# Branch B's weight folds: a block-diagonal matmul replaced by 32x32 tiles of the array, a turn on VectorE and a block exchange through DRAM

## The chip, the cores and the metric

The kernel runs on one core of one Trainium2 chip. The metric is the device time in microseconds of the whole program, as a median over several runs. A core has five engines with a queue each, and each works through its own list strictly in the order of the program: TensorE (PE, matmuls; its weight loads are listed as PEld), VectorE (DVE), ScalarE (ACT), GpSimd (POOL) and SyncE (SP, which here only issues DMAs). Matmul results lie in PSUM, which GpSimd and DMAs do not use here; all else lies in SBUF (128 partitions) or DRAM.

## The reference

Two attention branches A and B work on the same `x` (2048 rows of 448) with different weights, and their outputs are mixed by a gate per row. Cut to what matters here, one branch is

```python
qkv = (x @ wqkv).reshape(B, S, 3, H, Dh)            # D = 448, H = 16 heads of Dh = 28
pq = jnp.einsum("bhsd,hdf->bhsf", q, w_phi)          # per head, 28 x 28
pk = jnp.einsum("bhsd,hdf->bhsf", k, w_phi)
phi_q = concat([softmax(pq), softmax(-pq)])
phi_k = concat([softmax(pk), softmax(-pk)])
kv = jnp.einsum("bhsf,bhsd->bhfd", phi_k, v);  z = phi_k summed over s
o = (phi_q @ kv) / (phi_q @ z + 1e-6)
branch = o @ wo
out = sigmoid(x @ gate_w) * A + (1 - sigmoid(x @ gate_w)) * B
```

Since `q` and `k` are used only through `w_phi`, the kernel never computes them. It multiplies the weights first: for each head, `wqkv`'s 448x28 columns of that head times the head's 28x28 `w_phi`. This product is called a fold. There are four: k and q of branch A, k and q of branch B. The folded weights, 448x448 each, then stand in for the raw ones in the projections of `x`.

## The kernel before, in words

**Precision.** Projections run on pairs of a high and a low part (`fp32r` each). The high part of a tensor is a ScalarE copy into `fp32r`, the low part is the original minus the high part (VectorE or GpSimd). The 448 input channels are held as three chunks of 128 and one of 64 that stands twice in a tile of 128 partitions.

**Stages.** `x` is worked in 8 units of 256 rows (`NU = 8`, loop variable `u`). A first loop over `u` runs branch A's keys and values: `proj` with the folded k weights `wk[0]` (L446), `k_shift` and `k_exp` for both softmaxes (L195 to L202), `k_sums` (L211, L212 on VectorE and L220 on GpSimd) for their normalisation, `proj` with the values' weights (L459), `v_out` (L228), and `kv_acc` (L245), which adds unit `u - 1` to the state on TensorE. In the gaps it prepares branch B's weights: the split of `wv` and of `wo` into high and low parts (L131, L134) and the folds. A second loop over `u` runs branch B's keys and values with `wk[1]` and `wvs[1]`, and at the same time branch A's queries: `q_front` (L272, L274) stores them to DRAM in another order (`qd`), `q_load` reads them back (`tq`), `q_exp0`, `q_min`, `q_exp1` make both softmaxes (L297, L305, L312), `q_turn` (L315) turns 32x32 blocks on VectorE, `num` (L327) multiplies with the state in 32x32 tiles, and `a_turn`, `n_rec`, `n_den`, `weights`, `n_mul`, `n_add` (L522, L339 to L369) divide and weigh. A last part, ordered by the table STEPS, does branch B's queries and the output.

**Order.** Nothing is scheduled: each engine executes in the order in which the code issues. An instruction that waits holds all later ones of its engine; so do SP's DMAs.

**PSUM.** `two_tile()` hands out three tiles of two banks in rotation. Every projection, each half of a fold and each half of a `num` takes one, and TensorE must wait until the user of three takings ago has been read.

**A fold before** (`fold`, L159). `load_wt` brings the transposed raw weights of 4 heads at a time as 112 partitions, in four groups `g`. `bd` holds, for both branches, `w_phi` of the 4 heads of each group as a 112x112 block diagonal (built once on VectorE, L399). For each chunk of 128 channels and each group a matmul has the raw weights as the stationary operand and `bd` as the moving one (L151): 16 matmuls with 112 moving columns, in two PSUM tiles. `fold_out` then takes the high part on ScalarE (L156) and the low part on VectorE (L157) right from PSUM.

Branch B's k fold stands at the end of `u == 3` in the first loop (L492) and works on `wtb[1]`; its q fold stands in the second loop at `u == 0` (L563), between the projections of k and v, and works on a tile `ctr`. Both tiles are shared: `wtb` also holds pieces of `wo` (7 pieces of 32 rows per head group, `wo_part`, L409; `high_wo`, `low_wo`, stored to `wod`) and later the turned queries. `wk[1]` is first used by the projection of the second loop's `u == 0`, `wq[1]` by that of its `u == 6`.

## Time and profile before

| what | value |
|---|---|
| median of 3 runs | 353.95 us (353.79 to 353.97) |
| the profiled execution's own time | 353.85 us |
| its span in the profile | 352.1 us |
| granted TensorE clock | 1.0 |
| busy: PE / PEld / DVE / ACT / POOL | 345.7 / 305.9 / 271.6 / 121.7 / 261.9 us |
| branch B's k fold, L151 from 58.27 to the next group's start | 3.60 us |
| branch B's q fold, L151 from 116.71 to the next group's start | 3.56 us |

All times inside a run are microseconds from the start of the span. A row of the timeline gives the start, the length, the engine, the line of the kernel, the operation, output and inputs by the program's names, their shapes, and how many instructions were merged; a bracket tells how long the engine stood idle just before and what released it. In the page's last parts a row gives a group's busy time and mean. A matmul in full fp32 leaves two records.

### The profile page before, as it was taken

Reading aid. Unit: us, or ns where it says so; the run is one execution under the profiler, and the core shown is the slowest. Engines: PE = TensorE matmul, PEld = TensorE weight load, DVE = VectorE, ACT = ScalarE, POOL = GpSimd, SP = SyncE. Lnnn points to the kernel's source line nnn. Section 1 sums busy time; section 2 is a strip of 40 time slices with the busy share of each in tenths; the row PEclk is TensorE's granted clock in tenths of the full one; section 3 lists DMA queues with packets and bytes.
Section 4 is the critical chain, followed back from the end, with each engine's and each line's share of the span. In section 5 each row is a group of like instructions: output and inputs, shape, how many; then the busy total and the mean of one; then the engine's idle time right before and its main releaser. Section 6 shows DMA issues by size and latency. Waiting matters only on the chain.

```text
span 352.1 us, 8447 instructions
## 1 busy us (share of the span) xinstructions
PE 345.7 (98%) x3599; PEld 305.9 (87%) x3599; DVE 271.6 (77%) x313; ACT 121.7 (35%) x172; POOL 261.9 (74%) x228
## 2 busy tenths in 40 slices
PE   8999999999999999999999999999999999999994
PEld 7999889988899988889898988889888888888993
DVE  4428763852878859799989889898999999988840
ACT  5524444335145242324414141421125445343330
POOL 2553799597777206998988888895779999999840
PEclk9999999999999999999999999999999999999999
DMA  8796225511950303132233313178770553654111
GB/s 237 230 327 181 104 75 171 188 58 65 266 161 10 107 6 108 54 106 87 73 104 108 92 67 106 55 254 299 209 201 35 182 158 92 176 155 130 54 53 52
DMA packets 33877, 45.75 MB, mean 130 GB/s; under 512 B 11424, under 2 KB 27152, under 8 KB 33552
## 3 DMA queue, kind: packets, MB, share of 16 engines
q1 hardware_dynamic: 28688, 41.09, 37.5%
q10 hardware_dynamic: 5152, 4.13, 3.7%
q8 instruction: 28, 0.46, 0.5%
q14 instruction: 9, 0.07, 0.1%
HBM read 27.29 MB, written 19.53 MB: 133 GB/s over the span
## 4 chain that ended last, share of the span: by engine, by line
PE 81%; POOL 9%; DVE 5%; issue 1%; DMA 1%; ACT 1%; SPq 0%; POOLq 0%; ACTq 0%; DVEq 0%
PE two L181 50%; PE out L774 17%; PE two L327 5%; POOL e L220 3%; PE kv L245 3%; PE two L151 3%; POOL xg L112 2%; PE two L390 2%; DMA wtb<-wos 1%; DVE sm L211 1%; POOL e L198 1%; POOL wvb L134 1%; PE kv L327 1%; DVE wva L705 1%; POOL wtb L134 1%
## 5 line engine op out<-in xcount | busy, mean ns | idle before, releaser
L181 PE MATMUL two<-wka,xg 128*128 128x448 f32 x352 | 73.7, 365 | 0.0
L181 PEld LDWEIGHTS two<-wka,xg 128*128 128x128 f32 x352 | 65.2, 188 | 5.6 <-issue 0.8
L220 POOL TENSOR_TENSOR e<-e,rs 128x896 f32<-128x896 f32 x32 | 53.8, 1703 | 18.8 <-DVE rs L212 18.8
L228 ACT ACTIVATE vs<-two 128x896 f32<-128x896 f32 x16 | 14.7, 922 | 92.1 <-PE two L181 92.1
L211 DVE TENSOR_REDUCE sm<-e 128x32 f32<-128x896 f32 x32 | 33.1, 1075 | 9.0 <-ACT e L202 9.0
L181 PE MATMUL two<-wva,xg 128*128 128x450 f32 x176 | 39.4, 374 | 0.0
L181 PE MATMUL two<-wqa,xg 128*128 128x448 f32 x176 | 37.9, 370 | 0.0
L181 PE MATMUL two<-wvb,xg 128*128 128x448 f32 x176 | 37.2, 366 | 0.0
L315 DVE STREAM_TRANSPOSE wtb<-xrb 128x2048 f32<-128x2048 f32 x16 | 36.6, 2288 | 0.0
L181 PE MATMUL two<-wkb,xg 128*128 128x448 f32 x176 | 36.5, 362 | 0.0
L198 POOL TENSOR_TENSOR e<-mx,e 128x896 f32<-128x896 f32 x16 | 27.2, 1703 | 12.4 <-DVE mx L197 12.3
L181 PEld LDWEIGHTS two<-wva,xg 128*128 128x128 f32 x176 | 33.2, 190 | 2.9
L181 PEld LDWEIGHTS two<-wqa,xg 128*128 128x128 f32 x176 | 32.5, 188 | 3.5 <-ACT vs L228 0.4
L202 ACT ACTIVATE e<-e 128x896 f32<-128x896 f32 x32 | 28.7, 946 | 19.5 <-POOL e L198 19.4
L181 PEld LDWEIGHTS two<-wvb,xg 128*128 128x128 f32 x176 | 33.0, 188 | 2.7
L181 PEld LDWEIGHTS two<-wkb,xg 128*128 128x128 f32 x176 | 33.0, 188 | 2.3
L774 PE MATMUL out<-wkb,e 128*128 128x448 f32 x154 | 34.7, 370 | 0.1
L774 PEld LDWEIGHTS out<-wkb,e 128*128 128x128 f32 x154 | 28.5, 188 | 4.1 <-issue 0.8
L305 POOL TENSOR_TENSOR xrb<-qmn,tq 128x896 f32<-128x896 f32 x16 | 28.2, 1760 | 3.5 <-issue 3.0
L365 POOL TENSOR_TENSOR wva<-wva,cdd 128x896 f32<-128x896 f32 (+1 forms) x12 | 26.5, 2210 | 0.8
L365 POOL TENSOR_TENSOR ctr<-ctr,cdd 128x896 f32<-128x896 f32 (+1 forms) x12 | 26.5, 2212 | 0.6
L272 DVE TENSOR_REDUCE qmx<-two 128x32 f32<-128x896 f32 x14 | 15.1, 1078 | 15.0 <-PE two L181 15.0
(106 smaller groups left out, 587.3 us busy)
## 6 DMA issues: line engine op xcount, KB each, us to landing
tq<-qd SPq DMA_DIRECT2D x16, 448.0 KB, 5.6
qd<-uq ACTq DMA_DIRECT2D x32, 112.0 KB, 3.1
qd<-uq SPq DMA_DIRECT2D x32, 112.0 KB, 2.1
od<-wva SPq DMA_DIRECT2D x8, 448.0 KB, 2.5
wqa<-od SPq DMA_DIRECT2D x8, 448.0 KB
out<-bd SPq DMA_DIRECT2D x15, 224.0 KB, 2.8
wod<-wtb SPq DMA_DIRECT2D x14, 224.0 KB, 3.2
xrb<-in_xt SPq DMA_DIRECT2D x2, 1024.0 KB
```

Source lines behind the costliest of these rows:

```text
L181: nc.tensor.matmul(ps[:, i, :n], x[:, xc, o:o + P], w[:, k, wc], start=j == 0, stop=j == 10)
L198: nc.gpsimd.tensor_tensor(e5[:, 1], mx[:, 1, :, :, None].to_broadcast([P, 2, H, DH]), e5[:, 0], OP.subtract)
L202: nc.scalar.activation(es[k][:, s], es[k][:, s], AF.Exp)
L211: nc.vector.tensor_reduce(sm[:, s], e[:, s].rearrange("p (h f) -> p h f", f=DH), AX.X, OP.add)
L220: nc.gpsimd.tensor_tensor(e3, e3, rs[:, s, :, None].to_broadcast([P, HA, DH]), OP.mult)
L228: nc.scalar.activation(v[:, :, :, :, :DH].rearrange("p w j q f -> p w (j q) f"), hb(ps[:, :, :D]), AF.Copy)
L272: nc.vector.tensor_reduce(mx, p4, AX.X, OP.max)
L305: nc.gpsimd.tensor_tensor(eq[:, 1, :, :, :DH], mn.rearrange("p c a -> p a c")[:, :, :, None].to_broadcast([P, 8, 4, DH]), tview(k), OP.sub ...
L315: nc.vector.transpose(wtb[k % 2], eq.rearrange("p s a c f -> p (s a c f)"))
L327: nc.tensor.matmul(banks[r][32 * g:32 * g + 32, 256 * s:256 * s + 256], kvt[b][32 * r:32 * r + 32, s, g], eT[32 * r:32 * r + 32, s, g], st ...
L365: nc.gpsimd.tensor_tensor(c3, c3, dd.to_broadcast([P, 8, hi - lo, DH]), OP.mult)
L774: nc.tensor.matmul(outs[t % 2][:, :D], (hi, lo)[x][:, c], w[:, c], start=x == 0 and n == 0 and c == 0, stop=x == 1 and c == 6)
```

## The change

Branch B's two folds are done in another way; branch A's stay as they were. `bd` shrinks to branch A. `load_strips` lays each head's 28 raw weight rows at a partition that is a multiple of 32 (four DMAs instead of one), and `wps` holds branch B's `w_phi` in the same four strips (four DMAs). `fold_strips` issues 16 matmuls, one on each 32x32 tile of the array: `w_phi` of one head is the stationary operand, 448 columns of raw weights move. The result has the head's features on the partitions; VectorE turns it in 32x32 blocks from PSUM to SBUF over the raw weights (two instructions), four DMAs write it to `td` in DRAM so that channels become rows, and three read it back with 128 channels on the partitions, 32 columns per head of which 28 are used. From there ScalarE makes the high part (`high_folded`) and GpSimd the low part (`low_folded`), one instruction each.

The places move too. The k fold's matmuls stay at the end of `u == 3`, its high part stands at the start of `u == 5` and its low part in `u == 5`. The q fold's matmuls go to the end of the first loop (`u == 7`), its high and low parts stand in `u == 0` of the second loop behind `k_exp`. Since the k fold now occupies `wtb[1]` for longer, pieces 2 and 3 of `wo` go from `u == 5` to `u == 6`, beside piece 6. The output buffers `obs` become two tiles.

```diff
+    td = [dram.tile([D, 512], F32, name=f"td{i}") for i in range(2)]
...
-    bd = wp_.tile([PF, 2, 4, PF], F32, name="bd")
+    bd = wp_.tile([PF, 4, PF], F32, name="bd")
+    wps = wp_.tile([P, D], F32, name="wps")
+    wps = wps[:, :8 * HP].rearrange("p (b g m) -> p b g m", b=2, g=4)
...
+    def load_strips(dst, src):
+        w, s = dst.rearrange("p (g c) -> p g c", g=4), src.rearrange("(g r f) c -> r f g c", g=4, f=DH)
+        for r in range(4):
+            nc.sync.dma_start(w[HP * r:HP * r + DH, :, :D], s[r][:, :, :D])
+        return dst
+
+    def fold_strips(b, wt, i):
+        w, t = wt.rearrange("p (g c) -> p g c", g=4), wt[:, :4 * D]
+        ts = [two_tile(), two_tile()]
+        for g in range(4):
+            for r in range(4):
+                nc.tensor.matmul(ts[r // 2][HP * g:HP * g + HP, r % 2, :D], wps[HP * r:HP * r + DH, b, g],
+                                 w[HP * r:HP * r + DH, g, :D], start=True, stop=True)
+        o = t.rearrange("p (j i w m) -> p i w j m", i=2, w=2, m=HP)
+        for j, ps in enumerate(ts):
+            nc.vector.transpose(o[:, j], ps[:, :, :D].rearrange("p w (j m) -> p w j m", m=HP))
+        for g in range(4):
+            nc.sync.dma_start(td[i][:, g * P:g * P + P].rearrange("(j t) x -> t j x", t=HP),
+                              t[HP * g:HP * g + HP].rearrange("t (j x) -> t j x", x=P))
+        d = wt.rearrange("p (c x) -> p c x", c=4)
+        nc.sync.dma_start(d[:, :3], td[i][:384].rearrange("(c p) x -> p c x", p=P))
+        for p in (0, 64):
+            nc.sync.dma_start(d[p:p + 64, 3], td[i][384:])
+
+    def folded(wt, dst):
+        return wt.rearrange("p (h m) -> p h m", m=HP)[:, :, :DH], [dst[:, i].rearrange("p c (h f) -> p (c h) f", f=DH) for i in range(2)]
+
+    def high_folded(wt, dst):
+        w, d = folded(wt, dst)
+        nc.scalar.activation(d[0], w, AF.Copy)
+
+    def low_folded(wt, dst, eng):
+        w, d = folded(wt, dst)
+        eng.tensor_tensor(d[1], w, d[0].bitcast(F32), OP.subtract)
...
     def wo_part(c):
-        t = wtb[c // 2 % 2]
+        t = wtb[c in (2, 3)]
...
-    WOS = {3: (0, 1), 5: (2, 3, 4, 5), 6: (6,)}
+    WOS = {3: (0, 1), 5: (4, 5), 6: (2, 3, 6)}
...
         if u == 5:
+            high_folded(wtb[1], wk[1])
...
         if u == 1:
-            wtkb = load_wt(wtb[1], wkt[1])
+            load_strips(wtb[1], wkt[1])
+            for r in range(4):
+                nc.sync.dma_start(wps[HP * r:HP * r + DH], wphi[DH * r:DH * r + DH])
...
         if u == 4:
-            load_wo(2, 3, 4, 5)
+            load_wo(4, 5)
         if u == 5:
-            load_wo(6)
+            low_folded(wtb[1], wk[1], nc.gpsimd)
+            load_wo(2, 3, 6)
...
-            wtqb = load_wt(mid.tile([P, 2048], F32, name="ctr"), wqt[1])
+            wtqb = load_strips(mid.tile([P, 2048], F32, name="ctr"), wqt[1])
         if u > 1:
             kv_acc(u - 1)
         if u == 3:
-            fold(1, wtkb, wk[1])
+            fold_strips(1, wtb[1], 0)
+        if u == 7:
+            fold_strips(1, wtqb, 1)
...
         if u == 0:
             state_turn(0)
             q_turn(m)
-            fold(1, wtqb, wq[1])
         pv = proj(u, wvs[1], two_tile())
         v_out(k, pv)
         k_exp(k)
-        if u > 0:
+        if u == 0:
+            high_folded(wtqb, wq[1])
+            low_folded(wtqb, wq[1], nc.gpsimd)
+        else:
             q_turn(m)
...
-    ob = wp_.tile([P, 2, D], F32, name="bd")
-    obs = [ob[:, i] for i in range(2)]
+    obs = [wp_.tile([P, D], F32, name=n) for n in ("bd", "wps")]
```

How the instructions stand on an engine is shown at three places. In the changed kernel the line numbers are higher (its L221 is L181 of before, L285 is L245, L260 is L220, L238 is L198, L137 is L134, L345 is L305, L384 is L344, L355 is L315, L341 is L301, L251 and L252 are L211 and L212, L558 is L512); buffer numbers in names differ too. First GpSimd in the first loop, from the low parts of `u == 5` to the normalisation that the state of unit 6 needs (`wtb` rows are pieces of `wo`, `e` rows the softmax of k, `xrb` the softmax of q). Before:

```order
L134 TENSOR_TENSOR wtb_122<-wtb_122 128x448 x2
L134 TENSOR_TENSOR wtb_121<-wtb_121 128x448 x2
L220 TENSOR_TENSOR e<-e,rs 128x896 x2
L198 TENSOR_TENSOR e<-mx,e 128x896
L134 TENSOR_TENSOR wtb_122<-wtb_122 128x448
L305 TENSOR_TENSOR xrb<-qmn,tq_129 128x32x28
L220 TENSOR_TENSOR e<-e,rs 128x896 x2
```

And in the changed kernel:

```order
L137 TENSOR_TENSOR wtb_123<-wtb_123 128x448 x2
L204 TENSOR_TENSOR wkb<-wtb_124,wkb 128x1792
L260 TENSOR_TENSOR e<-e,rs 128x896 x2
L238 TENSOR_TENSOR e<-mx,e 128x896
L137 TENSOR_TENSOR wtb_124<-wtb_124 128x448 x2
L137 TENSOR_TENSOR wtb_123<-wtb_123 128x448
L345 TENSOR_TENSOR xrb<-qmn,tq_131 128x32x28
L260 TENSOR_TENSOR e<-e,rs 128x896 x2
```

The k fold's low part (L204) has taken the place of pieces 2 and 3 of `wo`, and these now stand with piece 6 between two normalisations.

Second VectorE at the end of the first loop and the start of the second, from `k_shift` of unit 7 on (`wtb` is the turned q of unit 0, `ctr` the turned fold). Before:

```order
L197 TENSOR_REDUCE mx<-e 128x32
L315 STREAM_TRANSPOSE wtb_121<-xrb 128x2048
L301 TENSOR_REDUCE qmn<-tq_130 128x32
L211 TENSOR_REDUCE sm<-e 128x32 x2
L212 RECIPROCAL rs<-sm 128x64
```

In the changed kernel:

```order
L237 TENSOR_REDUCE mx<-e 128x32
L186 STREAM_TRANSPOSE ctr<-two_1169 128x2x14x32
L186 STREAM_TRANSPOSE ctr<-two_1170 128x2x14x32
L355 STREAM_TRANSPOSE wtb_123<-xrb 128x2048
L341 TENSOR_REDUCE qmn<-tq_132 128x32
L251 TENSOR_REDUCE sm<-e 128x32 x2
L252 RECIPROCAL rs<-sm 128x64
```

The q fold's two transposes stand ahead of the turn of q and of the sums of unit 7.

Third ScalarE in the second loop's `u == 0` (`wka` is where the q fold's result goes, `glog` the gates). Before:

```order
L250 ACTIVATE kvs_75<-kv 128x8x28
L156 ACTIVATE wka<-two_1263 128x896
L156 ACTIVATE wka<-two_1274 128x896
L228 ACTIVATE vs_147<-two_1285 128x32x28
L202 ACTIVATE e<-e 128x896 x2
L512 ACTIVATE glog<-glog 128x16
```

In the changed kernel:

```order
L290 ACTIVATE kvs_75<-kv 128x8x28
L268 ACTIVATE vs_150<-two_1310 128x32x28
L242 ACTIVATE e<-e 128x896 x2
L200 ACTIVATE wka<-ctr 128x1792
L558 ACTIVATE glog<-glog 128x16
```

The high part, before two instructions ahead of `v_out`, is now one between the exponentials and the gates. On TensorE the q fold's 16 matmuls stand directly behind the state of unit 6, where before they stood behind that of unit 7; on GpSimd the q fold's low part stands ahead of the first division of the second loop (L384), where nothing stood.

More of the change, by code (lines that the diff above doesn't have):

```diff
@@ L157, in fold_out, with fold @@
         nc.vector.tensor_tensor(dl, ps[:, :, :D], dh.bitcast(F32), OP.subtract)
-    def fold(b, wt, dst):
+    def fold(wt, dst):
         for c in range(0, 4, 2):
@@ L398, in hedgehog_mix @@
     for q in range(4):
[L399 removed]
+        nc.vector.tensor_scalar(bd[:, :, q * DH:(q + 1) * DH], wp[:, 0, :, :DH], mask[:, q:q + 1], None, op0=OP.mult)
     pv = proj(0, wvs[0], two_tile(), TERMS0)
@@ L403, in hedgehog_mix @@
     v_out(0, pv)
-    fold(0, wt, wk[0])
+    fold(wt, wk[0])
     split_x(1, 0, 4, 0, 1, 2)
@@ L452, in hedgehog_mix @@
         if u == 1:
-            fold(0, wtqa, wq[0])
+            fold(wtqa, wq[0])
             k_sums(0)
```

7 lines of the change are left out of this document (3 added, 4 removed).

## The prediction

> **What bounds the kernel now.** First the page: the engines' busy shares and the chain that ended last.
>
> ```profile
> PE 345.7 (98%) x3599; PEld 305.9 (87%) x3599; DVE 271.6 (77%) x313; ACT 121.7 (35%) x172; POOL 261.9 (74%) x228
> ...
> PE 81%; POOL 9%; DVE 5%; issue 1%; DMA 1%; ACT 1%; SPq 0%; POOLq 0%; ACTq 0%; DVEq 0%
> ```
>
> TensorE is never idle for long, so whatever shortens its list shortens the run, as long as nothing else becomes late. Next, TensorE in order of time around both folds of branch B (L151) and behind them (columns: start, length, engine, line):
>
> ```profile
> 58.27 3.83 PE L151 MATMUL two<-bd,wtb 112*128 112x112 f32 x32
> 61.87 4.65 PE L181 MATMUL two<-wka,xg 128*128 128x448 f32 x22
> ...
> 105.73 0.99 PE L245 MATMUL kv<-e,vs 128*29 128x56 f32 x64
> 106.65 4.75 PE L181 MATMUL two<-wqa,xg 128*128 128x448 f32 x22
> 111.24 4.58 PE L181 MATMUL two<-wkb,xg 128*128 128x448 f32 x22
> 115.75 0.99 PE L245 MATMUL kv<-e,vs 128*29 128x56 f32 x64
> 116.71 3.80 PE L151 MATMUL two<-bd,ctr 112*128 112x112 f32 x32
> 120.27 4.72 PE L181 MATMUL two<-wvb,xg 128*128 128x448 f32 x22
> 124.93 1.49 PE L327 MATMUL two<-wtb,kvt 32*32 32x256 f32 x64
> 126.35 4.74 PE L181 MATMUL two<-wqa,xg 128*128 128x448 f32 x22
> ...
> 139.91 1.50 PE L327 MATMUL two<-wtb,kvt 32*32 32x256 f32 x64
> 141.33 0.99 PE L245 MATMUL kv<-e,vs 128*29 128x56 f32 x64
> ```
>
> From start to start the folds take 3.60 and 3.56 us (a group's printed length runs a little past the next start). The kv groups (L245) are the places where TensorE takes what GpSimd made: call the ones at 105.73 and 115.75 kv(6) and kv(7). So third, GpSimd up to them:
>
> ```profile
> 47.43 3.52 POOL L112 TENSOR_TENSOR xg<-xrb,xg 128x1536 fp32r<-128x1536 f32 x1
> ...
> 85.15 4.51 POOL L134 TENSOR_TENSOR wtb<-wtb 128x448 fp32r<-128x448 f32 x4 [2.37 <-ACT wtb L131]
> 91.89 3.37 POOL L220 TENSOR_TENSOR e<-e,rs 128x896 f32<-128x896 f32 x2 [2.23 <-DVE rs L212]
> ...
> 99.33 1.16 POOL L134 TENSOR_TENSOR wtb<-wtb 128x448 fp32r<-128x448 f32 x1 [2.41 <-ACT wtb L131]
> 100.45 1.76 POOL L305 TENSOR_TENSOR xrb<-qmn,tq 128x896 f32<-128x896 f32 x1
> 102.17 3.37 POOL L220 TENSOR_TENSOR e<-e,rs 128x896 f32<-128x896 f32 x2
> 111.03 3.36 POOL L220 TENSOR_TENSOR e<-e,rs 128x896 f32<-128x896 f32 x2 [1.27 <-DVE rs L212]
> ...
> 131.13 0.36 POOL L344 TENSOR_TENSOR cdd<-wva,crs 128x64 f32<-128x64 f32 x1 [9.74 <-DVE crs L339]
> 131.57 0.25 POOL L345 TENSOR_TENSOR cden<-cdd 128x32 f32<-128x32 f32 x1
> ```
>
> GpSimd ends its part for kv(6) at 105.54 and TensorE starts at 105.73: 0.2 us in hand. For kv(7) it is 114.39 against 115.75, 1.4 us. TensorE is the bound, but its suppliers are close behind here.
>
> **A fold on TensorE.** Removed: 16 matmuls with 112 moving columns. Added: 16 with 448, one on each 32x32 tile. The num group (L327) has the same form, two matmuls of 256 columns on each tile, two records each. Two short windows of it, up to 125.1 and up to 125.36:
>
> ```profile
> 124.93 0.50 PE L327 MATMUL two<-wtb,kvt 32*32 32x256 f32 x16
> 124.93 0.71 PE L327 MATMUL two<-wtb,kvt 32*32 32x256 f32 x32
> ```
>
> Sixteen records, one per tile, span 0.50 us, and the next sixteen add 0.21. At 448 columns a set adds 0.37, so one matmul on each tile spans 0.71 + 2 x 0.16 = 1.03. I take 1.0. Below it lies 0.71 (width costs nothing), above it 3.56 (tiles don't overlap, as before). That is 2.6 us less in the first fold and 2.55 in the second, 5.1 in all, if nothing else is late.
>
> The Trainium skill, TensorEngine Tiling (Array Packing), Performance Considerations, warns that tiling speeds up TensorE but not the emptying of PSUM, and says to use ScalarE and VectorE both for that; the change gives it to VectorE alone. By the rule the saving is lost behind VectorE. The rows of the second fold, below, agree.
>
> **The first fold.** VectorE used to wait for ScalarE there and do two subtractions; now it does two transposes right behind the matmuls, 1.06 each (L522 below, 2.31 for 2 x 1024 columns, at 896). So VectorE, ScalarE and GpSimd move up with TensorE, 2.6 us. ScalarE's new copy of the folded weights reads what went through DRAM:
>
> ```profile
> qd<-uq SPq DMA_DIRECT2D x32, 112.0 KB, 2.1
> tq<-qd SPq DMA_DIRECT2D x16, 448.0 KB, 5.6
> 81.17 0.92 ACT L228 ACTIVATE vs<-two 128x896 f32<-128x896 f32 x1 [5.93 <-PE two L181]
> 62.95 1.91 ACT L108 ACTIVATE xg<-xrb 128x2048 fp32r<-128x2048 f32 x1
> ```
>
> Out and back at 2.1 to 5.6 us each, with seven issues at about 0.4, is 7 to 14 us: ready at 69 to 76 for an engine that idles 5.93 us before 81.17 (78.6 when moved up). Its 1.67 us (1.91 x 1792/2048) is hidden there; without that cover they would delay the exponentials by as much. The subtraction on GpSimd (1792 columns) costs 4.1 by L112; bounds 3.4 (L220 x2) and 4.5 (L134 x4, the same columns). It replaces pieces 2 and 3 of wo at 85.15, so the gap of 2.23 covers it: 82.55 + 2.25 + 4.1 = 88.9, needed at 89.3.
>
> **Pieces 2 and 3 of wo** now stand with piece 6 ahead of kv(6), and nothing covers them. GpSimd may start when ScalarE has the first piece, 99.33 - 2.6 = 96.73. Three pieces at 1.13: 100.12. L305 (1.72 to the next start): 101.84. L220 twice: 105.2. TensorE is there at 105.73 - 2.6 = 103.13 and **waits 2.2 us**; kv(6) starts at 105.3. The first fold's gain is spent to 0.4.
>
> **The second fold** now follows kv(6). VectorE comes in order: the transposes stand ahead of L315 and of the sums that kv(7) needs, which before ran while TensorE worked.
>
> ```profile
> 104.59 2.30 DVE L315 STREAM_TRANSPOSE wtb<-xrb 128x2048 f32<-128x2048 f32 x1
> 106.82 1.04 DVE L301 TENSOR_REDUCE qmn<-tq 128x32 f32<-128x896 f32 x1
> 108.22 2.08 DVE L211 TENSOR_REDUCE sm<-e 128x32 f32<-128x896 f32 x2 [0.36 <-ACT e L202]
> 110.33 0.55 DVE L212 RECIPROCAL rs<-sm 128x64 f32<-128x64 f32 x1
> ...
> 120.54 0.92 ACT L156 ACTIVATE wka<-two 128x896 fp32r<-128x896 f32 x1 [0.87 <-PE two L151]
> ```
>
> kv(6) 105.3 + 0.92 = 106.2; fold to 107.2; its reader 0.27 later (as 120.54 follows 120.27): 107.5. Transposes 109.6, L315 111.85, L301 112.9, L211 115.0, L212 and hand-over 0.70: 115.7, L220 119.1. TensorE, after two projections (9.10), is ready at 116.3 and **waits 2.9 us**; kv(7) starts at 119.2. Its 0.96 gives 120.15 for the next projection, against 120.27 behind the old fold. Both gains, 5.15, have shrunk to 0.1.
>
> **Behind it.** In the first stage of branch B ScalarE's copy now stands ahead of the gates (L512), and GpSimd's 4.1 us ahead of L344.
>
> ```profile
> 127.53 0.20 ACT L512 ACTIVATE glog<-glog 128x16 f32<-128x16 f32 x1
> 127.77 0.18 DVE L513 TENSOR_SCALAR glog<-glog 128x16 f32<-128x16 f32 x1 [4.06 <-ACT glog L512]
> 128.15 2.31 DVE L522 STREAM_TRANSPOSE wva<-two 128x1024 f32<-128x1024 f32 x2
> 131.91 0.34 DVE L352 RECIPROCAL cden<-cden 128x32 f32<-128x32 f32 x1
> 137.94 1.09 DVE L196 TENSOR_TENSOR e<-two,mx 128x896 f32<-128x896 f32 x1
> ...
> 148.07 0.35 DVE L352 RECIPROCAL cden<-cden 128x32 f32<-128x32 f32 x1 [1.90 <-POOL cden L345]
> ```
>
> L512: 127.53 - 0.1 + 1.67 = 129.1, and VectorE, which waits for it (4.06), runs 1.5 late; behind it stand the transposes that free num's tiles, and all sums of the stage. GpSimd's subtraction runs 129.1 to 133.2, then L344 and L345: 134.0, so L352 is 2.1 late, and with it L196, which frees a PSUM tile that num writes: 140.0 + 1.09 = 141.1. TensorE would begin that num group at 139.8 and be through at 141.2. Its third matmul is held until 141.2: it **waits 1.4 us**, is through at 142.6, and kv(8) starts there against 141.33, 1.3 us later than before. GpSimd, with L220 released at 139.2, is done at 142.6 too. From there it is caught up: VectorE idles 1.90 in the next stage alone (148.07), and TensorE sets the pace again. So 1.3 us stay to the end.
>
> **SP's queue** is in order, and the change puts 24 more issues on it. (a) At the start four strips and four pieces of w_phi stand where one load stood, ahead of wo's copy; at 0.4 us each that copy starts some 3 us later, and pieces 0 and 1 of it are GpSimd's work only behind the strips' own fold at 58: covered. (b) The first fold's seven DMAs wait for the transposes (61.7) and for each other's landing, so the loads of pieces 4 and 5 leave SP at 69 to 76; GpSimd takes them at 85.15 - 2.6 = 82.55. (c) The loads of pieces 2, 3 and 6 wait for the subtraction (88.9), and the strips of the second fold stand behind them: out by 92, and even at twice 5.6 us there at 103, TensorE asks at 106.2. (d) The second fold's trip, back at 116.6 to 123.6, may hold SP past the time at which VectorE has turned to the stage's q (115.6 and on); q's store and load may so land as late as 123.6 + 2.1 + 5.6 = 131.3. ScalarE would begin on them at 129.3, but what follows waits for GpSimd's L305 behind 134.0. ScalarE itself asks for the folded weights at 127.4, after 123.6. All four lie beside other work; (d) has the least in hand.
>
> **Sum**, against the profiled execution's 353.85 us (0.1 below the median): -2.6 - 2.55 + 2.2 + 2.9 is -0.1 with the decimals kept, + 1.4 is +1.3: 355.15; on the median's scale **355.2 us**.
>
> **Rivals.** (1) The saving passes whole: 353.95 - 5.1 = 348.9; the 98% and the unbroken chain speak for it, the 0.2 us in hand at kv(6) against. Its likelier form is the single mechanism that GpSimd is in time for kv(6), because the wo pieces reach it before 94.5 or cost under 0.4 each: the 2.2 us are not lost, 353.0, faster. Nothing in the rows makes them so cheap: 7%. (2) The fold is cheaper than 1.0. Each us of a fold counts once at kv(6) and once at kv(7), so 0.71 gives 354.6. Together with the low ends of the other prices the run ends inside the bound of no change, 353.2 to 354.7: 16%. If sixteen tiles cut the old fold to a sixteenth, 3.56 / 16 = 0.22, the run would be 353.6; L327's 0.71 for a narrower set speaks against it: 2 of the 16%. The Trainium skill, TensorEngine Tiling (Array Packing), Overview, names up to 16 times as the theoretical most for 32x32 tiles; no row here comes near it. (3) The tiles don't overlap, the change doesn't do what it says: folds of 3.56, 355.2 + 5.1 = 360.3; L327 speaks against it: 4%. (4) The DRAM trip of the second fold comes back after 127.4 (rows of 512 bytes, bunched with other traffic); then L512, and all behind it, is as late again: 2 us late gives 357.2. It takes a trip of 20 us against the 14 at the upper row, so 11%, all other delays that I don't name among them.
>
> **How the numbers follow.** The forecast itself, 354.7 to 356.2, has 62%. A measurement of this kernel can tell about 0.2%, 0.7 us, from no change. Slower: 62 + 4 + 11 = 77%; same 16%; faster 7%. The range 353.7 to 357.0 leaves out the far ends of (1), (3) and (4) and part of (2); inside it lie the bounds of the subtraction (-0.2, +0.4) and half of those of the fold.
>
> **What would show it.** Right: fold groups of about 1.0 us; a wait of TensorE at kv(6) put down to GpSimd's L220 line, one near 3 us at kv(7), one at the second num; VectorE idle for 4 to 5 us before the second fold's transposes; L513 waiting longer for ScalarE. Wrong: fold groups near 3.5; kv(6) at 103; ScalarE waiting for a DMA at its copy; TensorE's list at 160 us no later than before.

## The result and the profile after

| kernel | median | against the kernel before on the same chip |
|---|---|---|
| before | 353.94 us | |
| changed | 364.98 us (363.93 to 365.85) | 1.031 (1.028 to 1.035) |

The change makes the kernel slower by 11.0 us. The forecast was 355.2 us: the sign was right, the size was not, and 365.0 lies far outside the range. The profiled execution took 364.21 us with a span of 362.4. Times in this document are medians over the runs of a kernel, and one run of the kernel with the gates first, 418.7 us at a mean granted clock of 0.75, is left out as a slow one. The page's busy time:

```profile
PE 344.9 (95%) x3599; PEld 301.9 (83%) x3599; DVE 274.2 (76%) x313; ACT 121.7 (34%) x170; POOL 269.9 (74%) x230
```

TensorE's share fell from 98 to 95%, and its busy time by only 0.8 us, although two folds of 3.6 us gave way to two of 1.4 and 1.7 us from start to start. So the rest of its work takes longer. The timeline of TensorE, first at the k fold, then from kv(6) on:

```profile
58.44 1.51 PE L182 MATMUL two<-wtb,wps 28*32 28x448 f32 x32
```

```profile
109.08 1.72 PE L285 MATMUL kv<-e,vs 128*29 128x56 f32 x64 [5.24 <-POOL e L260]
110.72 1.81 PE L182 MATMUL two<-ctr,wps 28*32 28x448 f32 x32
112.46 5.10 PE L221 MATMUL two<-wqa,xg 128*128 128x448 f32 x22
117.40 4.57 PE L221 MATMUL two<-wkb,xg 128*128 128x448 f32 x22
124.59 0.99 PE L285 MATMUL kv<-e,vs 128*29 128x56 f32 x64 [2.62 <-POOL e L260]
125.51 4.74 PE L221 MATMUL two<-wvb,xg 128*128 128x448 f32 x22
...
140.04 6.27 PE L221 MATMUL two<-wkb,xg 128*128 128x448 f32 x22 [3.69 <-DVE wva L568]
...
152.14 0.99 PE L285 MATMUL kv<-e,vs 128*29 128x56 f32 x64
```

Both folds are short, as meant. Then kv(6) starts at 109.08 against 105.73 before, kv(7) at 124.59 against 115.75, and kv(8), the last row, at 152.14 against 141.33. Nearly all of these 10.8 us stay to the end: the spans differ by 10.3. Three waits are new, 5.24, 2.62 and 3.69 us, and several groups are longer than their like: kv(6) 1.72 instead of 0.99, the q fold 1.81, a projection 6.27 instead of 4.57.

What released the first wait: GpSimd and ScalarE ahead of kv(6) (L137 and L134 are the low and high parts of a piece of `wo`).

```profile
85.38 4.05 POOL L204 TENSOR_TENSOR wkb<-wtb,wkb 128x1792 fp32r<-128x1792 f32 x1
...
97.35 1.16 POOL L137 TENSOR_TENSOR wtb<-wtb 128x448 fp32r<-128x448 f32 x1 [2.42 <-ACT wtb L134]
100.42 1.15 POOL L137 TENSOR_TENSOR wtb<-wtb 128x448 fp32r<-128x448 f32 x1 [1.91 <-ACT wtb L134]
102.85 1.15 POOL L137 TENSOR_TENSOR wtb<-wtb 128x448 fp32r<-128x448 f32 x1 [1.29 <-ACT wtb L134]
...
105.67 3.35 POOL L260 TENSOR_TENSOR e<-e,rs 128x896 f32<-128x896 f32 x2
```

```profile
99.76 0.58 ACT L134 ACTIVATE wtb<-wtb 128x448 fp32r<-128x448 f32 x1 [2.54 <-DMA wtb<-wos]
102.19 0.58 ACT L134 ACTIVATE wtb<-wtb 128x448 fp32r<-128x448 f32 x1 [1.85 <-DMA wtb<-wos]
```

GpSimd takes the first piece at 97.35, near the 96.73 of the prediction. But the second and third come 3.1 and 2.4 us apart, because ScalarE waits for their loads; the prediction had the three one behind another at 1.13 us. That is 3.2 us of kv(6).

The third wait, on VectorE and GpSimd:

```profile
134.60 3.99 DVE L559 TENSOR_SCALAR glog<-glog 128x16 f32<-128x16 f32 x1 [5.64 <-ACT glog L558]
...
138.80 2.31 DVE L568 STREAM_TRANSPOSE wva<-two 128x1024 f32<-128x1024 f32 x2
```

```profile
134.56 4.00 POOL L204 TENSOR_TENSOR wka<-ctr,wka 128x1792 fp32r<-128x1792 f32 x1 [5.95 <-ACT wka L200]
```

The gates' plus-1 on 128x16 numbers took 3.99 us; in the kernel before it took 0.18. It began 0.04 us behind GpSimd's low part of the q weights and ended with it. The transposes behind it (L568) free the PSUM tile for which TensorE waits until 140.04.

Last, two stretches of two us with the granted clock (the column before the last two; PE's busy time comes first behind the length):

```profile
108.00:110.00 2.00, 0.93 (x40) 0.93 (x44) 0.00 (x0) 0.00 (x0) 2.00 (x2) 0.50 0.89 290
...
142.00:144.00 2.00, 2.00 (x7) 1.76 (x6) 1.97 (x4) 0.00 (x0) 1.65 (x3) 0.51 0.00 0
```

Before, the clock was 1.00 in every stretch. Now it is 0.50 from 108 to 112 us, about the end of the 5.24 us wait, and 0.51 behind the 3.69 us wait. A matmul of the q fold lasts 0.95 us there, one of the k fold, of the same shape and at a clock of 1.00, lasts 0.53. Behind the 2.62 us wait the clock stays at 1.00.

### The profile page after: what moved, and what is told of

It is laid out like the page before. It is cut to its first block, busy times and chain, and to the rows that moved or that the text cites. A ratio compares the mean times of both kernels' runs of the same rounds, so it can differ in the third digit from the quotient of the medians.

```text
span 362.4 us, 8503 instructions
## 1 busy us (share of the span) xinstructions
PE 344.9 (95%) x3599; PEld 301.9 (83%) x3599; DVE 274.2 (76%) x313; ACT 121.7 (34%) x170; POOL 269.9 (74%) x230
## 4 chain that ended last, share of the span: by engine, by line
PE 80%; DVE 6%; DMA 5%; POOL 4%; issue 3%; ACT 1%; SPq 1%; POOLq 0%; DVEq 0%; ACTq 0%
PE two L221 51%; PE out L821 16%; PE two L367 5%; PE kv L285 3%; DMA wtb<-wos 3%; PE two L154 2%; POOL e L260 2%; PE two L430 2%; DMA wod<-wtb 1%; POOL wkb L204 1%; DVE glog L559 1%; PE kv L367 1%; DVE wtb L355 1%; DVE wva L752 1%; DVE qmn L341 1%
## 5 line engine op out<-in xcount | busy, mean ns | idle before, releaser
L221 PE MATMUL two<-wka,xg 128*128 128x448 f32 x352 | 73.8, 366 | 0.0
L221 PEld LDWEIGHTS two<-wka,xg 128*128 128x128 f32 x352 | 65.1, 188 | 6.4 <-issue 0.8
L260 POOL TENSOR_TENSOR e<-e,rs 128x896 f32<-128x896 f32 x32 | 53.8, 1703 | 15.0 <-DVE rs L252 15.0
L221 PE MATMUL two<-wkb,xg 128*128 128x448 f32 x176 | 38.3, 374 | 3.7 <-DVE wva L568 3.7
L221 PEld LDWEIGHTS two<-wkb,xg 128*128 128x128 f32 x176 | 34.3, 195 | 6.6 <-DVE wva L568 4.1
L251 DVE TENSOR_REDUCE sm<-e 128x32 f32<-128x896 f32 x32 | 33.0, 1073 | 8.6 <-ACT e L242 8.6
L221 PE MATMUL two<-wva,xg 128*128 128x450 f32 x176 | 39.4, 374 | 0.0
L221 PE MATMUL two<-wqa,xg 128*128 128x448 f32 x176 | 38.2, 372 | 0.0
L221 PE MATMUL two<-wvb,xg 128*128 128x448 f32 x176 | 37.2, 366 | 0.0
L221 PEld LDWEIGHTS two<-wqa,xg 128*128 128x128 f32 x176 | 32.8, 190 | 4.8 <-ACT e L242 1.5
L355 DVE STREAM_TRANSPOSE wtb<-xrb 128x2048 f32<-128x2048 f32 x16 | 36.6, 2289 | 0.3 <-issue 0.3
L345 POOL TENSOR_TENSOR xrb<-qmn,tq 128x896 f32<-128x896 f32 x16 | 28.2, 1760 | 10.5 <-ACT xrb L337 7.9
L221 PEld LDWEIGHTS two<-wva,xg 128*128 128x128 f32 x176 | 33.3, 190 | 2.9
L221 PEld LDWEIGHTS two<-wvb,xg 128*128 128x128 f32 x176 | 33.0, 188 | 2.8
L238 POOL TENSOR_TENSOR e<-mx,e 128x896 f32<-128x896 f32 x16 | 27.2, 1702 | 9.6 <-DVE mx L237 9.4
L352 ACT ACTIVATE xrb<-xrb 128x896 f32<-128x896 f32 x16 | 15.2, 951 | 35.0 <-POOL xrb L345 35.0
```

The costliest lines, as they stand in the source:

```text
L221: nc.tensor.matmul(ps[:, i, :n], x[:, xc, o:o + P], w[:, k, wc], start=j == 0, stop=j == 10)
L238: nc.gpsimd.tensor_tensor(e5[:, 1], mx[:, 1, :, :, None].to_broadcast([P, 2, H, DH]), e5[:, 0], OP.subtract)
L251: nc.vector.tensor_reduce(sm[:, s], e[:, s].rearrange("p (h f) -> p h f", f=DH), AX.X, OP.add)
L260: nc.gpsimd.tensor_tensor(e3, e3, rs[:, s, :, None].to_broadcast([P, HA, DH]), OP.mult)
L345: nc.gpsimd.tensor_tensor(eq[:, 1, :, :, :DH], mn.rearrange("p c a -> p a c")[:, :, :, None].to_broadcast([P, 8, 4, DH]), tview(k), OP.sub ...
L352: nc.scalar.activation(eq[:, 1, :, :, :DH], eq[:, 1, :, :, :DH], AF.Exp)
```

## The experiments

The theory after the result has three parts beside the waits that the prediction found in the order of work: **W**, the loads of wo pieces 2, 3 and 6 run on few DMA engines, one behind another (its rival **S**: other transfers hold them up); **G**, VectorE's plus-1 is held while GpSimd subtracts; **C**, TensorE's clock halves behind its waits. The edits shift the line numbers of some rows by a few.

### The gates first

```diff
         if u == 0:
+            gates()
             high_folded(wtqb, wq[1])
...
-        if u == 0:
-            gates()
-        else:
+        if u > 0:
             kv_acc(k - 1)
```

> The changed kernel with the gates (exponential on ScalarE, plus 1 and reciprocal on VectorE) put ahead of branch B's q weights' high copy and low part; nothing else moved. Theory G (the 128x16 plus-1 instruction took 3.99 us instead of 0.18 because VectorE was held while GpSimd ran its 4.00 us subtraction): the instruction now runs near 131 us, before the subtraction, and takes about 0.2 us; the transposes of the first sums follow the first num at once, and the 3.7 us wait of TensorE ahead of k projection 9 goes, with part of the slow clock that followed it (about 1 to 1.8 us). Time 359.5 to 361.5 us. Rival (the wait comes from the order alone, from the late weights or from the clock, and the long record is only a late release): the wait is paid at another place behind it, and the time stays within 0.7 us of the changed kernel's 365.0.

Measured: 360.5 us, 1.018 (1.016 to 1.020) of before. As theory G had it, 4.5 us less than the changed kernel; the rival's 365 is out. How long the plus-1 then takes is shown under Both.

### The pieces' loads in four DMAs each

```diff
-            nc.sync.dma_start(wo_part(c)[0], wos[:, HP * c:HP * (c + 1), :])
+            for g in (range(4) if c in (2, 3, 6) else (slice(0, 4),)):
+                p = slice(HP * g, HP * g + HP) if g in range(4) else slice(0, P)
+                nc.sync.dma_start(wo_part(c)[0][p], wos[g, HP * c:HP * (c + 1)])
```

> The changed kernel with the loads of wo pieces 2, 3 and 6 split into four DMAs of 32 partitions each. Theory W (each of these loads ran on about four DMA engines, one load behind another, 2.4 us apart, and the last landed at about 102 us): all three land by 98 us, ScalarE's copies stand one behind another from 96.7 us, GpSimd's low parts from 97.3 us, its products end near 105.9 instead of 109.1, and the wait of TensorE at kv(6) falls from 5.2 to about 2.1 us, which is what the prediction had for the order alone. Time 360.5 to 362 us, with the clock between 100 and 120 us back by a part. Rival (the pieces are late because the strips of the q weights and other transfers share the DMA engines, or because they are issued late at all): the last piece still lands past 100 us and the time stays within 0.7 us of 365.0.

Measured: 362.2 us, 1.024 (1.019 to 1.030), just above what was expected. ScalarE, GpSimd and TensorE in this kernel:

```profile
96.90 1.03 ACT L134 ACTIVATE wtb<-wtb 128x448 fp32r<-128x448 f32 x2
98.15 0.58 ACT L134 ACTIVATE wtb<-wtb 128x448 fp32r<-128x448 f32 x1 [0.22 <-DMA wtb<-wos]
```

```profile
97.59 3.39 POOL L137 TENSOR_TENSOR wtb<-wtb 128x448 fp32r<-128x448 f32 x3 [2.42 <-ACT wtb L134]
```

```profile
106.06 1.72 PE L285 MATMUL kv<-e,vs 128*29 128x56 f32 x64 [2.01 <-POOL e L260]
```

The three low parts stand one behind another, and the wait at kv(6) is 2.01 us, where the prediction had 2.2 for the order alone. But this edit changes two things. The pieces are spread over more DMA engines, and since SP needs 5.7 us for twelve issues, the strips of the q weights behind them leave at 95.5 instead of 91.2 us. The next run keeps the second and undoes the first.

### The strips later, the pieces as they were

```diff
-            wtqb = load_strips(mid.tile([P, 2048], F32, name="ctr"), wqt[1])
+            wtqb = mid.tile([P, 2048], F32, name="ctr")
...
             q_load(FRONTS[u - 1])
+            if u == 6:
+                load_strips(wtqb, wqt[1])
```

> The changed kernel with one move: the loads of the q weights' strips stand on SP behind the load of q 1, so that they leave at about 95 us as they do in the kernel with wide pieces, and not at 91.2; pieces 2, 3 and 6 stay one load each. The kernel with wide pieces changed two things, the spread of the pieces and (through SP's longer issue) the start of the strips; this run leaves the first as it was. Theory W alone (a piece takes 2.4 us on about four engines whatever else is moved, one behind another): the last piece still comes at about 102 us, TensorE waits 4.8 us or more at kv(6), and the time stays within 0.7 us of 365.0. Theory S (the strips take the engines on which the pieces run, and so hold them up): the pieces come 2.4 us apart from about 93.5 us, the last before 99.5 us, the wait is 2 to 2.8 us and the time 361.5 to 363 us.

Measured: 362.1 us, 1.023 (1.021 to 1.025). The strips left even later than meant, at 100.7. ScalarE and TensorE:

```profile
96.72 1.05 ACT L134 ACTIVATE wtb<-wtb 128x448 fp32r<-128x448 f32 x2
99.62 0.58 ACT L134 ACTIVATE wtb<-wtb 128x448 fp32r<-128x448 f32 x1 [1.84 <-DMA wtb<-wos]
```

```profile
106.52 1.65 PE L285 MATMUL kv<-e,vs 128*29 128x56 f32 x64 [2.62 <-POOL e L260]
```

The last piece comes at 99.62 instead of 102.19, and the wait is 2.62 instead of 5.24. So theory W alone falls: of the 3.2 us that the prediction missed at kv(6), 2.6 come from what SP issued behind the pieces, and 0.6 are left for the narrow loads (2.62 against 2.01). Behind the pieces stand the strips and, after them, the store of q 1, which left at 93.8 us in the changed kernel and at 91.4 here; the strips are most of these bytes (784 of 1008 KB), but their part alone isn't measured. Both are seen in the stretches of two us (DMA's share of 16 engines is the last column but one), first of the changed kernel, with the strips under way and behind them, then of this one:

```profile
94.00:96.00 2.00, 2.00 (x67) 1.84 (x55) 0.05 (x1) 1.91 (x4) 0.93 (x1) 1.00 0.97 168
96.00:98.00 2.00, 2.00 (x12) 1.88 (x11) 2.00 (x2) 1.22 (x2) 0.65 (x1) 1.00 1.01 160
...
100.00:102.00 2.00, 2.00 (x11) 1.84 (x10) 1.93 (x3) 0.34 (x1) 1.15 (x1) 1.00 0.27 97
```

```profile
96.00:98.00 2.00, 2.00 (x11) 1.88 (x10) 1.99 (x2) 1.77 (x3) 0.58 (x1) 1.00 0.26 97
```

With the strips all 16 engines are busy from 94 to 98 us; a piece alone takes a share of 0.26 to 0.27, 4.3 engines, and 97 GB/s. Loads that were issued behind the pieces took the engines on which the pieces ran, as theory S had it. The Trainium skill, DMA: Bandwidth & Descriptors, in the section on why a DMA increments its semaphore by 16, says that a transfer is spread over the largest number up to 16 that divides the slowest dimension of both its patterns; these loads read `[4, 32, 448]`, which by that rule gives 4, and the trace agrees.

### Both

> Both edits: the gates first and the three pieces' loads in four DMAs each. If the prediction's own sum was right but for these two and the clock that falls behind them, the time is its 355.2 us plus about 0.5 us for the k fold (1.5 instead of 1.0 us) and what is left of the slow clock: 355.5 to 357.5 us, slower than before by 0.4 to 1.0 per cent. If a third loss is hidden behind the two, it stays above 358.

Measured: 359.0 us, 1.013 (1.010 to 1.017). That is above the range that was expected, and above the 358 us past which a third loss was to be looked for. VectorE's plus-1 now, in front of the subtraction:

```profile
132.24 0.17 DVE L561 TENSOR_SCALAR glog<-glog 128x16 f32<-128x16 f32 x1 [6.22 <-ACT glog L560]
```

It is back at 0.17 us. What is left shows on TensorE and in its clock:

```profile
105.55 0.99 PE L285 MATMUL kv<-e,vs 128*29 128x56 f32 x64 [1.99 <-POOL e L260]
106.47 1.81 PE L182 MATMUL two<-ctr,wps 28*32 28x448 f32 x32
108.21 5.51 PE L221 MATMUL two<-wqa,xg 128*128 128x448 f32 x22
...
121.20 1.72 PE L285 MATMUL kv<-e,vs 128*29 128x56 f32 x64 [3.08 <-POOL e L260]
122.85 6.62 PE L221 MATMUL two<-wvb,xg 128*128 128x448 f32 x22
```

```profile
122.00:124.00 2.00, 2.00 (x43) 1.77 (x36) 1.66 (x3) 0.36 (x1) 0.82 (x1) 0.50 0.74 227
```

kv(6) starts at 105.55, where the prediction had 105.3, and the wait at kv(7) is 3.08 against its 2.9. But behind the two waits the same work takes longer: q fold 1.81, projections 5.51 and 6.62 for 4.6. The clock is 0.62 and 0.52 in the stretches from 106 to 110 us and about 0.50 from 122 to 126.

### The k fold issued twice

```diff
-        for g in range(4):
+        for g in (0, 1, 2, 3) * (1 + (i == 0)):
             for r in range(4):
                 nc.tensor.matmul(ts[r // 2][HP * g:HP * g + HP, r % 2, :D], wps[HP * r:HP * r + DH, b, g],
```

> The changed kernel with the 32 matmuls of the k fold issued a second time behind the first, into the same places. The second pass has no waits of its own: it costs what the tiles cost. Prediction: 1.0 us (bounds 0.71 to 3.56). Theory S (the first pass takes 1.45 us because it waits for eight loads one after another among its first matmuls): the stretch grows from 1.45 to 2.2 to 2.5 us. If tiles themselves take 1.45 us, it grows to 2.9. The whole time grows by that, or by less as kv(6) waits for GpSimd anyway.

Measured: one run, 365.2 us, and on TensorE

```profile
58.51 2.56 PE L182 MATMUL two<-wtb,wps 28*32 28x448 f32 x64
```

The second pass adds 2.56 - 1.51 = 1.05 us. So 16 tiles with 448 columns cost what the prediction took, 1.0, and the 0.45 above it belong to the first pass alone. There the queue of TensorE's weight loads holds six semaphore instructions between 58.3 and 58.9 us, the last of them 0.4 us into the fold; the q fold of the kernel with the waits filled (below), which takes 1.05 us, has two, and both stand ahead of it. That fits theory S, waits for the fold's eight loads one after another, though no run here takes these waits away.

### One fold alone

In the first kernel only the k fold is new, in the second only the q fold; the other fold, its loads and its part of `bd` are as they were before the change, and in the second so are `wo`'s pieces.

```diff
-        if u == 7:
-            fold_strips(1, wtqb, 1)
...
             q_turn(m)
+            fold(wtqb, wq[1], 1)
         pv = proj(u, wvs[1], two_tile())
```

> Only branch B's k fold is new (strips, tiles, blocks through DRAM, high copy and low part, wo pieces 2 and 3 behind it); its q fold stays as it was, 16 wide matmuls in the second pass. The prediction: 2.6 us less for the fold and 2.2 us more for the wait at kv(6): about 353.6 us, no change. Theory W (pieces on few DMA engines, then the slow clock): kv(6) waits 5.2 us for GpSimd as in the changed kernel, the clock halves behind it, kv(6) starts near 109 us against 105.7, and the time is 357.5 to 359.5 us.

```diff
-    WOS = {3: (0, 1), 5: (4, 5), 6: (2, 3, 6)}
+    WOS = {3: (0, 1), 5: (2, 3, 4, 5), 6: (6,)}
...
-            fold_strips(1, wtb[1], 0)
+            fold(wtkb, wk[1], 1)
```

> Only branch B's q fold is new; its k fold stays as it was, and wo pieces 2 and 3 are loaded and split where they were before the change. The prediction: 2.55 us less for the fold, 2.9 us more for the wait at kv(7), 1.4 us at the second num: about 355.7 us. Theory G with the clock: the wait at kv(7) and behind it the gates held by GpSimd's 4 us subtraction, k projection 9 late by 3.7 us and a halved clock behind that: 359 to 361.5 us. If the two halves of the change add up, this and the k fold alone together lose as much as the whole change, 11 us.

Measured: the k fold alone 358.5 us, 1.014 (1.012 to 1.015); the q fold alone 361.1 us, 1.021 (1.017 to 1.024). Their losses, 4.6 and 7.2 us, sum to 11.9, about the 11.0 of the whole. In the first, TensorE at kv(6) and behind it:

```profile
107.78 1.72 PE L285 MATMUL kv<-e,vs 128*29 128x56 f32 x64 [4.18 <-POOL e L260]
109.42 6.61 PE L221 MATMUL two<-wqa,xg 128*128 128x448 f32 x22
```

In the second, VectorE at the gates:

```profile
132.40 4.00 DVE L558 TENSOR_SCALAR glog<-glog 128x16 f32<-128x16 f32 x1 [8.05 <-ACT glog L557]
```

Each half has its own trouble: the k fold the late pieces, the q fold the held gates, and both the slow clock behind them. In the first the wait is 4.2 us and not 5.2; there the raw q weights come as one load and not as four strips behind the pieces.

### The waits filled

The kernel with both edits, and idle matmuls on TensorE in its two waits:

```diff
         b, u = divmod(k, NU)
+        for _ in range({6: 8, 7: 15}.get(k, 0)):
+            nc.tensor.matmul(kvb[:, 1, :D], wq[0][:, 0, 0, :P], wq[0][:, 0, 0], start=True, stop=True)
```

> The kernel with both edits (gates first, pieces in four DMAs each) and beside them idle matmuls of 128x448 into an unused bank: 8 ahead of kv(6) and 15 ahead of kv(7), 1.7 and 3.1 us of work at full clock, in the stretches in which TensorE waits for GpSimd anyway. Theory C (the 3.5 us that the kernel with both edits still lies above the prediction are the halved clock behind the waits): the granted clock stays 1.00 from 100 to 130 us, the q fold takes 1.0 us and not 1.8, kv(8) starts near 143.5 to 144.5 instead of 147.3, and the time is 355 to 356.3 us against 359.0. Rival (the waits themselves or the DRAM trip make the rest): the idle matmuls change nothing or cost their own time, 359 us or more.

Measured: 356.9 us, 1.008 (1.006 to 1.010), 2.1 us less with 23 matmuls more. The stretches and the q fold:

```profile
100.00:110.00 10.00, 9.62 (x135) 7.88 (x134) 4.59 (x5) 3.72 (x5) 7.32 (x5) 1.00 0.77 233
...
120.00:130.00 10.00, 9.20 (x161) 7.73 (x162) 5.82 (x8) 3.85 (x6) 2.74 (x4) 1.00 0.45 131
```

```profile
106.63 1.05 PE L182 MATMUL two<-ctr,wps 28*32 28x448 f32 x32
```

Work that nobody uses makes the kernel faster, because it keeps the clock at 1.00: theory C is shown, though the time is 0.6 us above its range. The runs of one kernel go with it: the q fold alone took 359.5 us at a mean clock of 0.995 and 362.8 at 0.981. The Trainium skill, TensorE: Matmul & The Clock Gate, states under What's actually happening that the clock is halved behind an idle window of some 3.4 us, and under Why this matters for your kernels it warns of gaps above about 3 us. The halving agrees; here a gap of 2.0 us brought it too (kv(6) of the kernel with both edits), so the measurement decides: two us can be enough. In the changed kernel the 2.62 us ahead of kv(7) did not, while 2.52 us at the same place of the q fold alone did: whether a gap of two to three us costs the clock isn't fixed by its length alone, and what else decides it no run shows.

### The stores of the pieces ahead of the load of q

What was left showed on VectorE and SP of the kernel with the waits filled:

```profile
111.39 2.31 DVE L357 STREAM_TRANSPOSE wtb<-xrb 128x2048 f32<-128x2048 f32 x1 [1.37 <-issue]
```

```profile
103.08 0.34 SPq L331 DMA_DIRECT2D tq<-qd  x1
103.52 0.38 SPq L468 DMA_DIRECT2D wod<-wtb  x1
```

The turn of q 0 writes over piece 6, whose stores stood on SP behind a load that did not leave before 103.08. Beside the edit below, the idle matmuls ahead of kv(7) are 11 and not 15, since the wait there should be shorter.

```diff
-            q_load(FRONTS[u - 1])
+            if u != 6:
+                q_load(FRONTS[u - 1])
...
             low_wo(c)
+        if u == 6:
+            q_load(1)
```

> The kernel with both edits and the waits filled, and one more move: on SP the load of q 1 stands behind the six stores of wo pieces 2, 3 and 6 and not ahead of them; the idle matmuls ahead of kv(7) are 11 in place of 15, since the wait there should be shorter. There SP sat waiting for the store of q 1 until 103.1 us, the stores of the pieces left from 103.5 to 107.1, and VectorE's turn of q 0, which writes into the tile that held piece 6, began at 111.4 instead of 110.0, 1.4 us late, with the sums for kv(7) behind it. Theory Q (this is the last piece of what the prediction had missed): the turn begins within 0.2 us of the end of the transposes, kv(7) starts near 119.4 instead of 120.8, kv(8) near 142.9, and the time is 355.2 to 356 us against 356.9. Rival (the turn waits for something else, or kv(7) for GpSimd anyway): the turn still starts near 111.4 and the time stays within 0.3 us of 356.9.

Measured: 355.6 us, 1.005 (1.004 to 1.006). VectorE and TensorE:

```profile
110.41 2.27 DVE L357 STREAM_TRANSPOSE wtb<-xrb 128x2048 f32<-128x2048 f32 x1
```

```profile
119.78 0.99 PE L287 MATMUL kv<-e,vs 128*29 128x56 f32 x64 [0.28 <-POOL e L260]
...
143.26 0.99 PE L287 MATMUL kv<-e,vs 128*29 128x56 f32 x64
```

The turn follows the transposes at once, kv(7) comes at 119.8 and kv(8) at 143.3. With four things put right that the prediction had not seen, its own sum, 355.2 us, is met within 0.4. A part of that is luck: against the kernel before on the same chip (353.7) this one is 1.9 us slower where the sum had 1.3, and its kv(6) starts at 106.2 and not at 105.3.

### The subtraction in quarters

To test G by its dose, the changed kernel with only this edit:

```diff
-            low_folded(wtqb, wq[1], nc.gpsimd)
+            for lo in range(0, 64, 16):
+                low_folded(wtqb, wq[1], nc.gpsimd, lo, lo + 16)
```

> The changed kernel with GpSimd's low part of the q weights in four subtractions of about 1.0 us in place of one of 4.0; all else, the place of the gates too, as it was. Theory G (an instruction of VectorE of this form is held while one of GpSimd's subtractions runs, and let go at that subtraction's end): the plus-1 of the gates lasts about 1 us, or a whole number of quarters where the next subtraction gets in first, in place of 3.99; with 1 us the wait ahead of k projection 9 falls from 3.7 to under 1 us and the time to 360 to 362 us. Rival (the long record has nothing to do with GpSimd's instruction): it stays at 4 us and the time at 365.

Measured: 360.6 us, 1.018 (1.017 to 1.020). VectorE and GpSimd:

```profile
136.11 1.14 DVE L560 TENSOR_SCALAR glog<-glog 128x16 f32<-128x16 f32 x1 [6.62 <-ACT glog L559]
```

```profile
136.06 4.47 POOL L205 TENSOR_TENSOR wka<-ctr,wka 128x448 fp32r<-128x448 f32 x4 [7.36 <-ACT wka L201]
```

With subtractions of 4.47 / 4 = 1.12 us the plus-1 lasts 1.14: it is let go at the end of the one that runs, though the next follows at once. That fits the Trainium skill, GPSIMD Engine Reference, Key points: GpSimd shares its SBUF interfaces with VectorE and contends with it where VectorE runs in a two-port mode or has two SBUF inputs. Which mode the plus-1 runs in no row shows; its price here is the whole rest of GpSimd's instruction.

### Both folds, the work around them moved

```diff
-    WOS = {3: (0, 1), 5: (4, 5), 6: (2, 3, 6)}
+    WOS = {3: (0, 1), 5: (4, 5, 2, 3), 6: (6,)}
...
+        if u == 5:
+            low_folded(wtb[1], wk[1], nc.vector)
+            load_wo(2, 3)
...
+            k_sums(7)
             q_turn(0)
...
         if u == 0:
             state_turn(0)
+        k_shift(k, pk)
...
+        if u == 0:
+            gates()
         k_exp(k)
+        if u == 0:
+            for lo in range(0, 64, 32):
+                high_folded(wtqb, wq[1], lo, lo + 32)
+                low_folded(wtqb, wq[1], nc.gpsimd, lo, lo + 32)
```

The first lines stand behind `k_shift`. Beside these, pieces 2, 3 and 6 come in four DMAs each, in `u == 0` the store of q from ScalarE stands behind `kv_acc` and the second exponential of q behind the copy of the state, and in `u == 1` `n_den` and `weights` stand behind `q_front`.

> Both folds new, the work around them moved so that nobody waits: the k weights' low part goes to VectorE behind the fifth k_shift, where VectorE is idle for 6 us, and wo pieces 2 and 3 (in four DMAs each) follow at once; the sums of k 7 come straight behind the q fold's transposes, ahead of the turn of q 0; the state's copy and turn come ahead of the eighth k_shift and of the second q exponential; the gates come ahead of the exponential of k 8; the q weights' high copy and low part run in two halves. What the theories say: the folds save 2.0 and 2.5 us of TensorE, and if all that was lost were the waits, the held gates and the clock, TensorE has no wait above 0.5 us from 90 to 160 us, the clock stays 1.00, kv(8) starts near 138 to 139 us against 141.3 before, and the time is 350 to 351.5 us, faster than before by about 1 per cent. If VectorE and GpSimd bound this stretch in any order, 353 to 355 us.

Measured: **349.4 us** (349.3 to 350.1), 0.988 (0.987 to 0.989) of before, faster than both kernels and a little faster than was expected. TensorE at kv(6) with the q fold behind it, and at kv(8):

```profile
104.29 0.99 PE L286 MATMUL kv<-e,vs 128*29 128x56 f32 x64 [0.19 <-POOL e L261]
105.21 1.05 PE L182 MATMUL two<-ctr,wps 28*32 28x448 f32 x32
...
137.39 0.99 PE L286 MATMUL kv<-e,vs 128*29 128x56 f32 x64
```

No wait above 0.5 us is left between 55 and 160 us, and kv(8) starts at 137.39 against 141.33. Of the 5.15 us that the prediction counted for the two folds 4.4 arrive.

### The order alone

The control: the kernel before, old folds, with those of these moves that can be made there (the sums of k 7, the state, the gates, the q store and exponential, `n_den` and `weights`).

> The kernel before, both folds as they were, with that part of the reordered kernel's moves which can be made there: the sums of k 7 ahead of the turn of q 0, the state's copy and turn earlier, the gates ahead of the exponential of k 8, the denominators of the first sums behind the third q difference. It tells whether the reordered kernel's 4.4 us come from the folds or from the order alone. If from the folds: 353.5 to 355 us here, as TensorE has nothing to wait for in the kernel before. If from the order: 350 to 352 us.

Measured: 354.6 us, 1.0018 (1.0009 to 1.0027). The order alone gains nothing, it costs 0.6 us. The reordered kernel's gain is the folds'. If these moves cost the same beside the new folds, which no run shows, the folds give 4.4 + 0.6 = 5.0 us by estimate.

## Why the prediction was wrong

Of the 9.8 us between 355.2 and 365.0 the series of kernels gives back: late pieces and held gates, with the slow clock behind them, 365.0 - 359.0 = 6.0 (2.8 and 4.5 when put right one at a time); the clock behind the waits that were left 2.1; the stores 1.4. The last 0.4 no run takes apart; the k fold's own 0.45 is about as large.

- **A fold on TensorE, 1.0 us**: right for the tiles, 1.05 in the q fold at full clock and in the second pass of the k fold. The k fold itself took 1.44 from start to start; a term for what its first matmuls lose was missing.
- **The small prices**: 4.05 and 4.00 us for the low part (4.1), 1.71 and 1.69 for the high part (1.67), 2.12 for two transposes (2.1; the row that it names, 2.31 for 2 x 1024 columns, gives 2.02): right.
- **The first fold's DRAM trip, 7 to 14 us, hidden**: it took 14.6 us from the end of the transposes to ScalarE's copy, a little past the range, and ScalarE did wait for it. The cover held by a hair, as the idle time ahead of the next copy shows:

```profile
76.88 1.71 ACT L200 ACTIVATE wkb<-wtb 128x1792 fp32r<-128x1792 f32 x1 [3.59 <-DMA wtb<-td]
79.18 0.92 ACT L268 ACTIVATE vs<-two 128x896 f32<-128x896 f32 x1 [0.59 <-PE two L221]
```

- **Pieces 2 and 3 of wo, a wait of 2.2 us at kv(6)**: this is the first step that failed. "Three pieces at 1.13: 100.12" takes the second and third piece as landed when GpSimd wants them. Part (c) of SP's queue asked when the strips land, at 103, and not what they do to the pieces issued ahead of them, nor what a piece's own load takes. With that put right the wait is 2.0, so the part that the order makes was sized rightly.
- **A wait of 2.9 us at kv(7)**: 2.62 in the changed kernel and 3.08 in the one with both edits, and both are near by luck. TensorE came to kv(7) later by the slow clock, and VectorE's chain was later too: in the one with both edits the turn of q 0 stood 1.18 us for the stores of piece 6, which the prediction's chain missed. In the kernel with the stores put right 2.7 us lie between the end of the second projection (117.07) and kv(7) (119.78), so the part that the order makes was sized rightly. The Trainium skill's warning that the emptying of PSUM may become the bottleneck (TensorEngine Tiling (Array Packing), Performance Considerations) fits a part of this wait, the two transposes' 2.1 us. But the saving need not be lost to it: in the reordered kernel VectorE alone empties both folds, and 4.4 of 5.15 us arrive.
- **Behind it, L512 1.5 us late and a wait of 1.4 us at the second num**: the second step that failed. L513 was taken at its 0.18 us beside a GpSimd that works for 4 us; it took 3.99. In the kernels without that hold the num wait is there, 0.90 us, behind `e` of VectorE as argued.
- **The clock**: the third step, one that the sum lacks. It took every TensorE row at the clock of 1.00 that the kernel before had while TensorE had no such wait, and then inserted waits of 2.2 and 2.9 us. These waits can bring the halved clock with them, and in the kernel with both edits it cost 2.1 us.
- **SP (d), the second trip**: right, ScalarE didn't wait for it. Rivals (1) to (4) did not come.

The range failed for a plain reason: it held bounds for the prices that were in the sum, and none for a transfer, an instruction or a clock that had been carried over from the kernel before as they were.

## What to carry to other kernels

In these kernels a wait of two us or more ahead of TensorE could cost more than its length, because the clock fell with it: a change that saves matmuls and adds such waits can end slower. Filling the gaps gave back 2.1 us; moving the late work away, with the pieces in four DMAs, turned a loss of 11.0 us into a gain of 4.4. When a load comes to stand close ahead of its user, price the load: its issue, how many DMA engines its pattern reaches, and the transfers that share them, those issued behind it too. Before a long GpSimd instruction is moved, look which short VectorE instructions will run beside it.

## What was not expected of the hardware

- A VectorE plus-1 on 128x16 fp32 numbers in SBUF took 3.99 us beside a 4.00 us subtraction of GpSimd, 1.14 us beside one of 1.12 us, and 0.17 us alone.
- TensorE's clock fell to about 0.5 behind gaps of 2.0 to 5.2 us, though not behind each of two to three us; 23 idle matmuls made the kernel 2.1 us faster.
- A load of 224 KB whose pattern begins with a dimension of 4 used 4.3 of 16 DMA engines; with the strips issued behind three such loads all 16 were busy for 4 us, and TensorE's wait for the last of the three was 2.6 us longer.
